# Log-sum rows of a two-pass attention: from four broadcast multiplies on VectorE to one small copy and four transfers

## The chip, the cores and the metric

The kernel runs on one core of a Trainium2 chip. The metric is the device time of one execution in microseconds. Five engines work side by side, each on its own list of instructions in written order: PE (TensorE, matmuls), DVE (VectorE), ACT (ScalarE), POOL (GpSimd) and SP (SyncE, which here only issues transfers). Matmuls write to PSUM, from which DVE and ACT take the results into SBUF. Semaphores order the engines against each other.

## The reference

Two attention layers, "A" and "B", each over its own input of 2048 tokens with 1024 features and 32 heads of 32; their outputs are concatenated.

```
def _B_ref(x, wqkv, wo):                      # "dense" units of the kernel
    B, S, D = x.shape
    H = 32; Dh = D // H; W = 256
    qkv = (x @ wqkv).reshape(B, S, 3, H, Dh).transpose(2, 0, 3, 1, 4)
    q, k, v = qkv[0], qkv[1], qkv[2]
    scores = jnp.einsum("bhqd,bhkd->bhqk", q, k) * (Dh ** -0.5)
    idx = jnp.arange(S)
    mask = (idx[:, None] - idx[None, :] >= 0) & (idx[:, None] - idx[None, :] < W)
    scores = jnp.where(mask[None, None], scores, -1e9)
    p = _softmax(scores, axis=-1)
    o = jnp.einsum("bhqk,bhkd->bhqd", p, v)
    return o.transpose(0, 2, 1, 3).reshape(B, S, D) @ wo
```

A query of layer B sees the last 256 keys, itself included. Layer A differs in the mask alone: a query sees 8 keys, two positions apart (itself, 2 back, ... 14 back). All data is float32.

## The kernel before

The work is cut into 8 units of 512 tokens: units 0 to 3 are layer B ("dense"), units 4 to 7 layer A ("window"). A unit has 8 head groups of 4 heads, numbered `hg = 8 * unit + s`. There are four kinds of work on PE: the projections to queries and keys (L518) and to values (L583), the output projection (L645), together "the gemm"; and attention. For precision, each float32 operand of the gemm is split into a high and a low part (`Stream.parts`, L195: copy at L201 or L204, difference at L207), and three products are summed.

Dense attention of one head group has two passes.

First pass (`first`, L846): for each of 4 heads and 4 blocks of 128 queries, the scores are computed with queries on the partitions (L857), masked and reduced to a maximum by DVE (L862), and put through an exponential on ACT that also sums them (L867). The scores' operands are "stacked": three copies of the 32 head dimensions, high and low parts, fill partitions 0 to 95 of `qst` and `kst`, so one matmul over 96 rows sums the three products.

Log-sum (`log_sum`, L878, and `rows`, L894): logarithm of the sums (L880), maximum minus logarithm (L885), again as high and low parts (L887, L888). One matmul with the identity (L896) turns these into 32 rows of 128 columns in PSUM: row 16a + 4j + b is part a of head j and query block b. `spread` (L898) brings these rows to partitions 96 to 127 of the stacked queries.

Second pass (`second`, L932): the scores are computed again, now with keys on the partitions (L940), and with the log-sum added by the matmul itself, since the contraction also runs over partitions 96 to 127, where the keys hold ones (`ones`, L338, written once at the start). An exponential (L947) gives the finished probabilities; two triangular masks are cut by POOL (L926) or DVE (L929), and the product with the values follows (L987), in two lots of key blocks. The result leaves PSUM at L822 and L826 and feeds the output projection of the unit.

Two copies of `qst` and `kst` alternate between head groups. The stacking transfers of group `hg` (L479, and L408 and L469 for the keys that a unit passes on to the next) wait until the second pass of group `hg - 2` is done. They are issued by SP, from buffers (`natp`, 3 of them) that the projection's results are put in (L455, L459).

The order of all instructions is made by a planner when the kernel is built (L1058 on). It has four lists, log-sum rows, second passes, first passes and gemm, and at each step takes the item that can start first; at a tie attention goes before gemm. Each list is in a fixed order: the gemm cannot skip an item that waits. The planner keeps a clock (`Clock`, L44) for each engine and for the transfers, from a table of durations; `ROWS_LATE`, `KEYS_LATE` and `SEAT_LATE` (L28, L29) are added to the clock times at which certain data is taken to be there. For a transfer by SP the clock books 1.34 us from issue to movement, and for the kind `part` 0.33 us of movement and 0.56 until it is seen (L50 to L54); SP itself is held 0.63 us. What the planner believes sets only the order; on the chip, semaphores set the times.

After the last two dense groups, `qst` and `kst` are taken over as buffers for the window units: `clear` (L808 on) zeroes them on POOL (L810, L814). It is called from `free_keys` (L785), when the last matmul of a second pass has been written. The window units have no log-sum rows; L711 and L774 are their scores and values.

## Time and profile before

| | |
|---|---|
| median of 3 runs | 1832.38 us (1831.74 to 1832.67) |
| profiled execution, span | 1830.6 us |
| PE busy | 1807.8 us (99%) |
| DVE busy | 1202.9 us (66%) |
| ACT busy | 889.4 us (49%) |
| POOL busy | 394.4 us (22%) |
| L902, the four multiplies of `spread` | 128 instructions, 79.3 us of DVE |
| transfers issued by SP | 544 |

The span is the time from the first to the last instruction of the profiled execution, 1.8 us (0.1%) below the median of the runs. PE's busy time covers a matmul from its start to a modelled end; matmuls overlap, so a mean duration of one (394 ns for 512 columns) is longer than the step from one to the next. A group's row has its line, engine, operation, output and inputs, the shapes, the count, then busy time and mean duration of one, then the idle time of the engine just before it and what ended that. "PEld" is the loading of a matmul's stationary operand.

### The profile page before, as it was taken

How to read it: one execution, taken by the hardware profiler on the slowest of the kernel's cores; microseconds unless marked ns; L12 is line 12 of the kernel's file. 1: busy time of each engine (PE TensorE's matmuls, PEld its weight loads, DVE VectorE, ACT ScalarE, POOL GpSimd, SP SyncE). 2: the span in 40 equal slices, each digit the busy share in tenths (PEclk: the TensorE clock that was granted, in tenths of full speed). 3: DMA queues.
4: the chain of work that ended last, by engine and by line, in shares of the span. 5: the costliest groups of instructions: out<-in, count | busy, mean ns of one | idle time of the engine just before them, and what ended most of it. 6: DMA issues, size and time to landing. Idle time of an engine off the chain costs nothing.

```text
span 1830.6 us, 38331 instructions
## 1 busy us (share of the span) xinstructions
PE 1807.8 (99%) x14826; PEld 1477.5 (81%) x14826; DVE 1202.9 (66%) x2694; ACT 889.4 (49%) x2254; POOL 394.4 (22%) x926
## 2 busy tenths in 40 slices
PE   9999999999999999999999999999999999999998
PEld 7787777888778888788887788888888788888887
DVE  6677886768867669777777564655547445655463
ACT  5556466565655655656555343433425234423331
POOL 3322323233242324332233200110001000100000
PEclk9999999999999999999999999999999999999999
DMA  8455665545656456455554343444334443534432
GB/s 242 121 138 139 176 164 150 170 121 160 164 155 164 136 151 183 125 157 141 141 142 130 110 135 116 152 143 130 119 115 143 133 138 108 162 107 128 127 104 83
DMA packets 109141, 257.43 MB, mean 141 GB/s; under 512 B 14496, under 2 KB 29856, under 8 KB 108960
## 3 DMA queue, kind: packets, MB, share of 16 engines
q0 software_dynamic: 41760, 152.06, 28.1%
q1 hardware_dynamic: 56832, 83.00, 17.6%
q10 hardware_dynamic: 10368, 19.93, 3.0%
q8 instruction: 117, 1.92, 0.5%
q14 instruction: 64, 0.52, 0.1%
HBM read 164.63 MB, written 23.07 MB: 103 GB/s over the span
## 4 chain that ended last, share of the span: by engine, by line
PE 92%; DVE 4%; DMA 2%; ACT 2%; issue 1%; SPq 0%; ACTq 0%; POOL 0%; DVEq 0%; POOLq 0%
PE g L518 37%; PE g L645 19%; PE g L583 17%; PE s L940 5%; PE s L857 5%; PE o L987 5%; PE s L711 2%; PE o L774 2%; DMA raw<-xs 1%; DVE w L207 1%; DVE s L862 1%; ACT s L867 0%; DMA qst<-nat 0%; DMA pbuf<-nat 0%; DVE x L207 0%
## 5 line engine op out<-in xcount | busy, mean ns | idle before, releaser
L518 PE MATMUL g<-x,w 128*128 128x512 f32 x3072 | 770.2, 394 | 3.8 <-DVE nm L729 2.4
L518 PEld LDWEIGHTS g<-x,w 128*128 128x128 f32 x3072 | 566.3, 189 | 114.2 <-issue 8.3
L583 PE MATMUL g<-w,x 128*128 128x256 f32 (+1 forms) x2304 | 391.9, 320 | 0.9 <-issue 0.7
L207 DVE TENSOR_TENSOR w<-raw,w 128x512 fp32r<-128x512 f32 x516 | 338.6, 698 | 52.0 <-ACT w L201 44.8
L583 PEld LDWEIGHTS g<-w,x 128*128 128x128 f32 x2304 | 332.3, 190 | 29.2 <-DVE w L207 1.8
L645 PE MATMUL g<-ot,w 128*128 128x512 f32 x1416 | 343.6, 393 | 3.7 <-DVE ot L826 1.8
L867 ACT ACTIVATE s<-s,nm 128x384 f32<-128x384 f32 (+2 forms) x512 | 274.3, 536 | 102.1 <-DVE nm L862 101.8
L862 DVE CUSTOM_DVE_ANT_0 s<-s,mask_d 128x384 f32<-128x384 f32 (+2 forms) x512 | 261.5, 553 | 88.2 <-PE s L857 87.5
L645 PEld LDWEIGHTS g<-ot,w 128*128 128x128 f32 x1416 | 262.4, 188 | 59.3 <-DVE ot L826 3.2
L926 POOL TENSOR_SCALAR_AFFINE_SELECT pbuf<-pbuf 128x128 f32<-128x128 f32 (+1 forms) x606 | 219.8, 391 | 325.1 <-ACT pbuf L947 323.8
L947 ACT ACTIVATE pbuf<-s 128x384 f32<-128x384 f32 (+2 forms) x480 | 202.7, 505 | 72.2 <-PE s L940 70.2
L159 POOL DMA_DIRECT2D raw<-wqk x126 | 68.1, 540 | 457.5 <-DVE w L207 356.3
L204 DVE CAST w<-raw 128x1024 fp32r<-128x1024 f32 x205 | 141.7, 691 | 24.8 <-PE g L518 24.0
L940 PEld LDWEIGHTS s<-qst,kst 128*128 128x128 f32 x704 | 113.0, 188 | 41.2 <-ACT s L867 16.3
L857 PE MATMUL s<-kst,qst 96*128 96x384 f32 (+2 forms) x512 | 142.4, 342 | 0.9 <-ACT s L867 0.6
L940 PE MATMUL s<-qst,kst 128*128 128x256 f32 (+2 forms) x704 | 136.5, 302 | 3.5 <-ACT s L867 3.0
L719 DVE TENSOR_TENSOR band<-s,near 128x160 f32<-128x160 f32 x128 | 32.4, 315 | 158.0 <-PE s L711 158.0
L536 ACT COPY ost<-g 128x512 f32<-128x512 f32 x54 | 31.7, 587 | 207.1 <-PE g L645 200.4
L857 PEld LDWEIGHTS s<-kst,qst 96*128 96x128 f32 x512 | 93.4, 189 | 26.2 <-issue 4.7
L826 DVE TENSOR_TENSOR ot<-o,ot 128x512 fp32r<-128x512 f32 x64 | 44.0, 688 | 101.6 <-ACT ot L822 101.4
L867 ACT ACTIVATION_READ_ACCUMULATOR s<-s,nm 128x1 f32 x512 | 105.3, 206 | 0.0
L159 POOL DMA_DIRECT2D raw<-wo x64 | 34.2, 534 | 304.2 <-DVE w L207 260.2
(77 smaller groups left out, 1298.6 us busy)
## 6 DMA issues: line engine op xcount, KB each, us to landing
raw<-wqk POOLq DMA_DIRECT2D x126, 512.0 KB, 4.3
raw<-wv POOLq DMA_DIRECT2D x72, 512.0 KB, 5.1
raw<-wo POOLq DMA_DIRECT2D x64, 512.0 KB, 4.1
qst<-nat SPq DMA_DIRECT2D x96, 256.0 KB, 5.3
kst<-nat SPq DMA_DIRECT2D x96, 256.0 KB, 5.6
raw<-xs POOLq DMA_DIRECT2D x28, 512.0 KB, 4.6
outs<-ost ACTq DMA_DIRECT2D x56, 256.0 KB, 2.3
kst<-halo SPq DMA_DIRECT2D x72, 128.0 KB, 4.5
```

Source lines behind the costliest of these rows:

```text
L159: (self.nc.scalar if early else self.nc.gpsimd).dma_start(raw if len(ap.shape) == 2 else raw.rearrange("p (a b) -> p a b", a=2), ap)
L204: nc.vector.tensor_copy(t[:, 0, :], raw)
L207: nc.vector.tensor_tensor(t[:, 1, c:c + 512], raw[:, c:c + 512], t[:, 0, c:c + 512].bitcast(F32), op=ALU.subtract)
L518: nc.tensor.matmul(h["ps"], h["w"][:, a, k * P:(k + 1) * P], xt[u][k][:, b, :], start=(k == 0 and i == 0), stop=(k == NK - 1 and i == 2))
L583: nc.tensor.matmul(ps, xt[u][kw * g + k][:, a, p0:p0 + P], h["w"][g][:, c, k], start=(first and t == 0 and half == 0), stop=(last and t == 2),
L645: nc.tensor.matmul(h["ps"], w[:, a, c:c + P], ot[u, k][:, b, :], start=(k == 0 and i == 0), stop=(k == NK - 1 and i == 2))
L857: nc.tensor.matmul(ps[:, :n], q[0:96, j, b * P:(b + 1) * P], kk[0:96, j, c0:c1], start=True, stop=True)
L862: nc.vector.tensor_tensor_reduce(ps[:, :n], ps[:, :n], mask[:, cut:full], scale=-1.0, scalar=BIG, op0=ALU.add, op1=ALU.min, accum_out=nm)
L867: nc.scalar.activation(ps[:, :n], ps[:, :n], AF.Exp, bias=nm, scale=-1.0, accum_out=sm)
L926: nc.gpsimd.affine_select(w, w, pattern=[[0, m], [step, n]], compare_op=ALU.is_ge, fill=0.0, base=base, channel_multiplier=chan)
L940: nc.tensor.matmul(ps[:, i * n:(i + 1) * n], kk[:, j, 256 + kb * P:256 + (kb + 1) * P], q[:, j, q0:q0 + n], start=True, stop=True)
L947: nc.scalar.activation(w, ps[:, :pack * n].rearrange("p (j n) -> p j n", j=pack), AF.Exp)
```

## The change

The rows of the log-sums leave PSUM by one copy of 32 x 128 elements into a new SBUF tile `row`, on ACT or DVE, whichever the planner's clock has free first. The PSUM bank is given back after that copy. Four transfers issued by SP, one for each head slot j, then each write all 32 rows of 128 as 8 rows of 512 (part and head, by 4 query blocks) into partitions 96 to 103 of the stacked queries' slot j. So each head's slot holds the rows of all four heads, where before DVE multiplied each slot by a pattern that left only its own head's row at its own block. The choice of the head moves to the keys: instead of ones in partitions 96 to 127, slot j of the stacked keys holds 1 in the two rows of head j (high and low part) and 0 in the others. The second pass contracts over 104 partitions in place of 128.

`ROWS_LATE` goes from 0 to 2.0: the planner takes the rows to be there 2 us after the transfer's booked landing. `clear` for the last dense group is called later, after its last product with the values has been written.

```
-ROWS_LATE, KEYS_LATE = 0, 1.2
+ROWS_LATE, KEYS_LATE = 2.0, 1.2
...
-        pick = cst["pick"] = pickp.tile([32, 16], F32, name="pick")
+        pick = cst["pick"] = pickp.tile([P, 16], F32, name="pick")[96:104, :4]
         nc.gpsimd.memset(pick, 0.0)
-        for row in (0, 16):
-            nc.gpsimd.affine_select(pick, pick, pattern=[[-1, 16]], compare_op=ALU.not_equal, fill=1.0, base=-row,
+        for row in (0, 4):
+            nc.gpsimd.affine_select(pick, pick, pattern=[[-1, 4]], compare_op=ALU.not_equal, fill=1.0, base=-row,
                                     channel_multiplier=1)
...
         def ones():
-            zero = cst["mask_d"][96:P, None, P:2 * P].to_broadcast([32, 24, P])
+            zero = cst["mask_d"][96:104, None, P:2 * P].to_broadcast([8, 6, P])
             for t in kst:
-                nc.scalar.activation(t[96:P, :, :].rearrange("p j (a s) -> p (j a) s", s=P), zero, AF.Identity,
-                                     bias=1.0, scale=1.0)
-                ck.use("act", 2.7, ck.now)
+                for j in range(4):
+                    nc.scalar.activation(t[96:104, j, :].rearrange("p (a s) -> p a s", s=P), zero, AF.Identity,
+                                         bias=cst["pick"][:, j:j + 1], scale=1.0)
+                    ck.use("act", 0.72, ck.now)
...
-        if hg >= last_dense - 1 and U * NG - 1 > last_dense:
+        if hg == last_dense - 1 and U * NG - 1 > last_dense:
             ck.defer(ck.now + 0.3, lambda: clear(hg % 2))
...
             def spread():
-
-                h["rows"] = []
-                for j in range(4):
-                    nc.vector.tensor_tensor(q[96:P, j, :].rearrange("p (b s) -> p b s", s=P),
-                                            ps[0:32, None, 0:P].to_broadcast([32, 4, P]),
-                                            cst["pick"][0:32, 4 * j:4 * j + 4, None].to_broadcast([32, 4, P]), op=ALU.mult)
-                    e = ck.use("dve", 0.61, ck.now)
-                    h["rows"].append(e + ROWS_LATE)
+                row = rowp.tile([32, P], F32R, tag="row", name="row")
+                if ck.ends("act", 0.22, ck.now) <= ck.ends("dve", 0.2, ck.now):
+                    nc.scalar.copy(row, ps[0:32, 0:P])
+                    e = ck.use("act", 0.22, ck.now)
+                else:
+                    nc.vector.tensor_copy(row, ps[0:32, 0:P])
+                    e = ck.use("dve", 0.2, ck.now)
                 rs.give(bank, e)
+
+                def place():
+                    h["rows"] = []
+                    for j in range(4):
+                        nc.sync.dma_start(q[96:104, j, :].rearrange("r (b s) -> r b s", s=P).bitcast(F32),
+                                          row.bitcast(F32))
+                        h["rows"].append(ck.copy("part", e, ck.now) + ROWS_LATE)
+
+                if hg < 2 or hg - 2 in done["second"]:
+                    place()
+                else:
+                    waiting.setdefault(hg - 2, []).append(place)
...
-                nc.tensor.matmul(ps[:, i * n:(i + 1) * n], kk[:, j, 256 + kb * P:256 + (kb + 1) * P],
-                                 q[:, j, q0:q0 + n], start=True, stop=True)
+                nc.tensor.matmul(ps[:, i * n:(i + 1) * n], kk[0:104, j, 256 + kb * P:256 + (kb + 1) * P],
+                                 q[0:104, j, q0:q0 + n], start=True, stop=True)
...
                 if hg == last_dense and ks[-1] == nk - 1:
+                    if U * NG - 1 > last_dense:
+                        clear(buf)
                     seat_free(hg)
```

More of the change, by code (lines that the diff above doesn't have):

```diff
@@ L229 @@
     pickp = ctx.enter_context(tc.tile_pool(name="pickp", bufs=1))
+    rowp = ctx.enter_context(tc.tile_pool(name="rowp", bufs=1))
     opool = ctx.enter_context(tc.tile_pool(name="opool", bufs=NO))
```

## The prediction

> **What bounds the kernel now.** I read the page's busy table first, then the busy time by stretches of the span, then who waited for whom, and last the timeline at the places where PE was not full.

> ```profile
> span 1830.6 us, 38331 instructions
> PE 1807.8 (99%) x14826; PEld 1477.5 (81%) x14826; DVE 1202.9 (66%) x2694; ACT 889.4 (49%) x2254; POOL 394.4 (22%) x926
> 0.00:1030.00 1030.00, 1018.34 (x6127) 820.91 (x6129) 762.47 (x1954) 596.15 (x1708) 317.18 (x785) 1.00 0.55 151
> 0.00:30.00 30.00, 27.03 (x96) 20.49 (x97) 16.52 (x25) 15.31 (x17) 12.12 (x32) 0.94 0.78 236
> 30.00:60.00 30.00, 29.81 (x139) 23.95 (x138) 23.16 (x76) 18.00 (x64) 6.42 (x17) 1.00 0.60 168
> 150.00:180.00 30.00, 26.86 (x152) 20.76 (x151) 24.18 (x76) 20.77 (x68) 7.11 (x19) 1.00 0.53 139
> 360.00:390.00 30.00, 30.00 (x209) 23.80 (x208) 20.35 (x51) 17.85 (x51) 8.28 (x24) 1.00 0.55 147
> 420.00:450.00 30.00, 30.00 (x204) 26.58 (x203) 27.50 (x64) 13.87 (x41) 8.04 (x16) 1.00 0.55 153
> 450.00:480.00 30.00, 29.04 (x176) 22.58 (x175) 25.99 (x68) 19.20 (x54) 13.62 (x28) 1.00 0.72 201
> 690.00:720.00 30.00, 28.83 (x208) 24.17 (x208) 28.12 (x68) 15.89 (x45) 12.76 (x23) 1.00 0.61 175
> ```

> In the rows of stretches the columns are the stretch, its length, and the busy time of PE, PEld, DVE, ACT and POOL, then PE's clock, the DMA share and GB/s. The dense units, which alone are changed, take the first 1030 us. PE is busy for 1018.34 of them: 11.66 us are idle, and 0.19 + 2.97 = 3.16 of these lie in the first 60 us, where the kernel starts. So an edit that takes work off the other engines can give back about 8.5 us that this view shows. In the middle of a unit (360 to 390) PE has no idle time at all and DVE has 10 us of it. Where one unit goes over into the next (420 to 450, 690 to 720, and 150 to 180 in the first) DVE is the full one: it splits the next unit's input there, and there PE has its few holes.

> [...]

> ```profile
> 1805.13 21.77 PE g L645 x96
> L902 DVE TENSOR_TENSOR qst<-s,pick x128: 672/674/686, 49.5 to 1013.8; 32x512 fp32r<-32x512 f32 x128
> PE s L896 <- DVE hl L888: 3.6, 4, 2.0
> ACT nat L455 <- DMA qst<-nat: 6.1, 3, 2.8
> ```

> The last two are waits: us in total, times, longest. Nobody is listed as waiting for L902, which the change removes. What PE does wait for is the step before it (L888), and an evacuation of PSUM waits for a stacking transfer (L455): there the gemm has run so far ahead that it needs attention to set a buffer free.

> **The change part by part.** *Matmuls.* As many as before, contracting over 104 rows in place of 128. The nearest rows on both sides of 104 are equal, so 0:

> ```profile
> L857 PE MATMUL s<-kst,qst 96*128 96x384 f32 x448 | 129.8, 351 | 0.9 <-ACT s L867 0.6
> L940 PE MATMUL s<-qst,kst 128*128 128x384 f32 x256 | 70.0, 350 | 0.2
> L438 SPq DMA_DIRECT2D pbuf<-nat x256: 467/544/1912, 1030.7 to 1768.8; - x128
> DMA to landing us min/median/max: 2.0/2.9/7.0
> L867 ACT ACTIVATE s<-s,nm 128x128 f32<-128x128 f32 x32 | 10.9, 340 | 13.0 <-DVE nm L862 13.0
> L880 ACT ACTIVATE ln<-sm 128x16 f32<-128x16 f32 x32 | 6.9, 216 | 0.8
> SPq L479 <- PE s L940: 336.0, 28, 27.5
> ```

> *DVE.* 128 instructions of 0.674 us go, four in each of 32 head groups: 2.5 us a group in one piece, 79 us in all (union). In return there is one copy of 32x128 out of PSUM for each group, on ACT or DVE, whichever the planner finds free. The trace has no such copy; it lies between ACT's 0.216 us (16 columns) and 0.340 (128 columns), and I take 0.3. ACT has 40% of its time free in these units: 0.

> *The four transfers.* SP issues 128 more, by L438's median 0.544 us each: 70 us in 1030. SP stood waiting for PE for 336 us in its stacking line alone, so the issue time is hidden. What they add is latency. A 16 KB transfer is not in the trace; the nearest is L438 (64 KB, same queue, also into some partitions of a tile), 2.0 to 7.0 us from issue to landing, median 2.9. I take 2.9 and keep both ends. The planner books 1.34 + 0.33 + 0.56 + 2.0 = 4.23 us from the end of the copy for the first and 0.63 more for each one after it, so PE's written order puts the second-pass scores (L940) later and gemm in the space. If the transfer lands within what is booked, PE loses nothing for as long as there is gemm. Queued behind the four on SP are the next stacking copies; they wait for the end of this very second pass (hg minus 2), so they are not delayed further by the queue.

> Where the gemm is held by attention, the longer path counts. Four places:

> ```profile
> 430.13 0.22 PE L896 MATMUL s<-ident,hl 128*32 128x128 f32 x1
> 432.74 0.34 PE L940 MATMUL s<-qst,kst 128*128 128x128 f32 x2
> 444.87 0.29 DVE L929 TENSOR_TENSOR pbuf<-pbuf,keep_d 128x128 f32<-128x128 f32 x1
> 494.53 0.22 PE L896 MATMUL s<-ident,hl 128*32 128x128 f32 x1
> 496.88 2.48 DVE L902 TENSOR_TENSOR qst<-s,pick 32x512 fp32r<-32x512 f32 x4
> 499.98 0.33 PE L940 MATMUL s<-qst,kst 128*128 128x128 f32 x2
> 1011.78 0.22 PE L896 MATMUL s<-ident,hl 128*32 128x128 f32 x1
> 1013.99 0.33 PE L940 MATMUL s<-qst,kst 128*128 128x128 f32 x2
> 1026.90 0.94 POOL L810 MEMSET band<- 128x1024 f32 x1
> 1027.79 1.91 POOL L814 MEMSET wide<- 128x2176 f32 x1
> 1029.66 1.11 POOL L926 TENSOR_SCALAR_AFFINE_SELECT pbuf<-pbuf 128x256 f32<-128x256 f32 x3
> 1031.92 0.50 PE L645 MATMUL g<-ot,w 128*128 128x512 f32 x1 [0.69 <-ACT ot L822]
> 160.17 0.22 PE L896 MATMUL s<-ident,hl 128*32 128x128 f32 x1
> 163.30 0.34 PE L940 MATMUL s<-qst,kst 128*128 128x384 f32 x1
> 178.47 0.22 PE L896 MATMUL s<-ident,hl 128*32 128x128 f32 x1 [1.99 <-DVE hl L888]
> ```

> From the rows matmul to the first paired second-pass matmul the new plan needs about 0.22 + 0.2 + 0.3 + 0.15 + 4.23 + 0.63 = 5.7 us (0.2 and 0.15 are the planner's own allowances), and 5.1 where the first item has one head, as in the first unit.
> (a) Head group 13, just before a unit's end: 2.6 us now, 3.1 more then. But its first masks come at 444.87, long after its exponentials, since DVE is full; they wait for DVE, which has 2.5 us less to do. Hidden: 0. The same at group 21.
> (b) Groups 15 and 23, whose output the next o-projection waits for: 5.45 us now, as L902 itself stands behind other DVE work until 496.88; 0.2 more then. 0.
> (c) Group 31: 2.2 us now, 3.5 more. Against that, the two memsets (0.94 + 1.91 = 2.85 us) no longer stand in front of its last three masks on POOL. Net 0.6, and PE already waits 0.7 there: +1.
> (d) The first unit, where attention and not gemm leads: group 4 takes 3.1 us now, 1.9 more then, and the next group on the same buffers follows it. +2, with at least 0 (DVE is 2.5 us shorter for each group, too) and at most 2 x 3.5 = +7.

> *What the lighter DVE gives back.* PE waits for L888, behind DVE's queue, 3.6 us in all, 2.0 of them at 178.47. I take 2.5 of these; the ends are 0 and the whole 8.5 us of idle time.

> *Other edits.* The rows' PSUM bank is free some 2 us sooner (bounded by the same 8.5 us; not counted twice). The constant rows of the keys take eight short ACT instructions in place of two at 24 us, where ACT is half idle: 0. The last memset comes later, but the windowed group that needs it starts after others: 0.

> The sum: 1830.6 + 1 + 2 - 2.5 = 1831.1 us for a profiled execution. The median of the runs shown, 1832.4, lies 1.8 above this profile; 1833 us is predicted. Less than 0.2% of the time, 3.7 us, is about what a measurement of this kernel can tell from no change.

> **The rivals.** *Slower: row transfers land later than booked.* PE executes in written order, so a late row stops the gemm behind it too. It happens where the rows come while the 256 KB stacking copies are still moving. Seven copies were issued from 455.24 to 460.06 and group 14's rows matmul ran at 462.93:

> ```profile
> 455.24 1.95 SPq L479 DMA_DIRECT2D qst<-nat  x3
> 460.06 0.54 SPq L469 DMA_DIRECT2D halo<-nat  x1
> 462.93 0.22 PE L896 MATMUL s<-ident,hl 128*32 128x128 f32 x1 [0.31 <-DVE hl L888]
> halo<-nat SPq DMA_DIRECT2D x1, 256.0 KB, 9.1
> ```

> The last of the seven landed 9.1 us after its issue, at 469.2, while the rows would be issued at 463.5. A transfer that needs 7.0 us in place of 2.9 lands 7.0 - 4.2 = 2.8 us after its booked time; at four unit ends 11 us, 1844 us in all. It decides once lateness at those places is over 0.9 us each. For it: the same queue and such traffic at each unit end. Against it: the planner counts the queue in its own clock, and in mid-unit the copies are done (360 to 390 has a DMA share of 0.55). [...]

> *Faster: DVE at the unit ends was the true limit.* With 2.5 us less of it in front of the input splits, masks and first-pass reductions, the holes close: at most the 8.5 us, with the +3 above hidden as well, so 1832.4 - 6 = 1826 with about two thirds given back. For it: DVE 27.5 and 28.12 of 30 us at two unit ends. Against it: PE lost only 0.96 and 1.17 us in the stretches around them.

> *No effect at all:* PE was full and stays full, and the small losses and gains cancel. This is the forecast, since DVE is off the path everywhere but at the unit ends.

> **How the numbers follow.** Within 0.2% (1829 to 1836): 0.38. Slower, by late rows: 0.35. Faster, by the DVE relief: 0.27. The range runs from 1823, near the floor set by the idle time, to 1848, the slower rival with two thirds as much again of its 11 us and a little; that leaves out some 0.05 below and 0.11 above. For the forecast alone it is 1829 to 1836.

> **What would show it.** Right: DVE's busy time in the dense units 80 us lower, L940's mean unchanged, SP with 128 more issues, and PE idle in the first 1030 us still 9 to 14 us. The slower rival: a wait of PE, or of its weight loads, on the transfer that writes qst from the row tile, above all at unit ends. The faster rival: PE idle at 150 to 180 us down from 3.1 us to about 1. Wrong in another way: since every booked time moves, the planner may write quite another order of PE's work, and holes may arise in places that now have none; the view of stretches would show them away from the four places above.

## The result and the profile after

The changed kernel takes 1857.3 us (median of 4 runs, 1855.2 to 1861.8) beside 1832.1 us of the kernel before in the same comparison. The ratio is 1.0142, with a 95% interval of 1.0128 to 1.0156: slower by 25 us, where 1833 us had been predicted, and outside the range that ended at 1848. In the changed kernel's own numbering L898 is the rows matmul, L903 and L906 are the new copy on ACT and DVE, L913 the four transfers, L953 the second-pass scores, L859 the first-pass scores, L520 and L585 the projections.

The page's span and busy table after:

```profile
span 1855.2 us, 38489 instructions
PE 1820.9 (98%) x14826; PEld 1484.4 (80%) x14826; DVE 1127.2 (61%) x2571; ACT 888.9 (48%) x2265; POOL 386.2 (21%) x948
```

DVE lost 1202.9 - 1127.2 = 75.7 us of work, and nobody gained by it. PE, with the same 14826 matmuls, is busy 13.1 us longer and idle 34.3 - 22.8 = 11.5 us longer. The busy time by stretches shows where. Columns: stretch, length, busy time of PE, PEld, DVE, ACT and POOL, then PE's clock, DMA share, GB/s. After:

```profile
0.00:1055.00 1055.00, 1031.53 (x6119) 827.72 (x6119) 686.00 (x1831) 595.43 (x1719) 308.20 (x809) 0.99 0.55 150
1055.00:1855.00 800.00, 789.39 (x8708) 656.67 (x8707) 441.21 (x740) 293.44 (x546) 78.01 (x140) 1.00 0.42 127
180.00:210.00 30.00, 26.55 (x172) 22.98 (x170) 22.55 (x61) 12.09 (x38) 9.04 (x19) 0.94 0.60 165
360.00:390.00 30.00, 29.02 (x170) 22.92 (x162) 18.09 (x48) 17.90 (x53) 6.58 (x19) 1.00 0.51 138
450.00:480.00 30.00, 27.41 (x175) 21.92 (x174) 23.73 (x59) 17.00 (x48) 12.09 (x24) 0.95 0.61 168
720.00:750.00 30.00, 27.41 (x154) 20.98 (x153) 21.52 (x59) 14.72 (x44) 7.06 (x15) 0.94 0.63 170
```

and the kernel before, its last 800 us:

```profile
1030.00:1830.00 800.00, 789.44 (x8703) 656.57 (x8697) 440.45 (x740) 293.20 (x546) 77.20 (x142) 1.00 0.42 127
```

The window units are the same to 0.1 us, so all of it lies in the dense units, which now end some 25 us later: 23.5 us of idle PE there in place of 11.7, and 1031.5 us of busy time in place of 1018.3. The holes are small and in many places. The loss grows unit by unit: measured at the evacuation of each unit's last keys, the kernel is 3.9, 10.7, 16.6 and 25.0 us behind the kernel before, and it ends 24.6 behind.

Who waits for whom: PE's waits for attention's work in the changed kernel, a selection (us in total, times, longest):

```profile
PE s L898 <- DVE hl L890: 4.2, 4, 1.9
PE s L859 <- DMA kst<-nat: 3.0, 2, 1.8
PE s L859 <- ACT s L869: 2.5, 4, 0.9
PE s L953 <- ACT s L869: 2.0, 1, 2.0
PE s L859 <- DMA qst<-row: 1.0, 1, 1.0
```

The new transfers are waited for once, for 1.0 us. What has changed is the order. PE's timeline at group 13, and SP's at the same time; the columns are start, length, engine, line, operation and, in brackets, the idle time before:

```profile
440.14 0.22 PE L898 MATMUL s<-ident,hl 128*32 128x128 f32 x1
440.20 1.62 PE L520 MATMUL g<-x,w 128*128 128x512 f32 x6
441.65 1.60 PE L585 MATMUL g<-w,x 128*128 128x256 f32 x12
443.09 0.86 PE L859 MATMUL s<-kst,qst 96*128 96x384 f32 x4
443.79 6.64 PE L585 MATMUL g<-w,x 128*128 128x256 f32 x54
450.26 0.56 PE L953 MATMUL s<-qst,kst 104*128 104x128 f32 x4
```

```profile
440.71 2.96 SPq L913 DMA_DIRECT2D qst<-row  x4
```

From the rows matmul to the second pass it is 450.26 - 440.14 = 10.1 us, in place of 2.6 before. PE stands still for none of it: four first-pass matmuls and 72 of the gemm (6 + 12 + 54) were written into the space. Over all 32 head groups, counted in the two traces, this way is 9.0 us on the mean in place of 3.3.

The other part of the loss is PE's clock. Stretches of 10 us in the changed kernel:

```profile
190.00:200.00 10.00, 7.98 (x44) 7.40 (x43) 8.60 (x26) 4.76 (x17) 4.10 (x7) 0.83 0.42 131
220.00:230.00 10.00, 10.00 (x44) 8.30 (x44) 7.75 (x27) 5.08 (x20) 0.83 (x2) 0.83 0.42 129
470.00:480.00 10.00, 8.06 (x48) 5.77 (x48) 7.72 (x20) 4.22 (x13) 1.77 (x2) 0.85 1.03 261
740.00:750.00 10.00, 10.00 (x40) 8.34 (x39) 7.35 (x18) 2.82 (x9) 1.61 (x2) 0.84 0.67 193
790.00:800.00 10.00, 9.52 (x54) 6.00 (x50) 5.44 (x19) 6.20 (x18) 3.57 (x11) 0.89 0.48 125
```

A clock of 0.83 over 10 us is 1.7 us of full clock lost. Behind each row stands one slot of 3.4 us at clock 0.50, from 193.7, 221.0, 477.0, 739.8 and 797.8; three of the rows cut their slot off. Five slots make 5 x 1.7 = 8.5 us. Apart from these, each of the two kernels has one such slot in the first 20 us, and the kernel before has no other in its dense units. So 11.8 us of the 25 are idle time and about 8.5 are matmuls at half the clock. Some 5 us are left, which lie in PE's busy time. Part of them comes with the pauses: the dense units have some 41 in place of 24, and before each the last matmul is counted as busy to its modelled end, 0.394 - 0.227 = 0.17 us beyond the step to the next (0.394 is the page's mean of one of 512 columns, 0.227 the 21.77 us of the 96 at the end of the kernel before, by 96), which makes an estimated 2.9 us. Of the last 2 the cause isn't known.

### The profile page after: what moved, and what is told of

Read it like the earlier page. It is cut to its first block, busy times and chain, and to the rows that moved or that the text cites. A ratio compares the mean times of both kernels' runs of the same rounds, so it can differ in the third digit from the quotient of the medians.

```text
span 1855.2 us, 38489 instructions
## 1 busy us (share of the span) xinstructions
PE 1820.9 (98%) x14826; PEld 1484.4 (80%) x14826; DVE 1127.2 (61%) x2571; ACT 888.9 (48%) x2265; POOL 386.2 (21%) x948
## 4 chain that ended last, share of the span: by engine, by line
PE 90%; DMA 3%; DVE 3%; ACT 2%; issue 1%; SPq 0%; ACTq 0%; POOL 0%; DVEq 0%; POOLq 0%
PE g L520 36%; PE g L647 18%; PE g L585 17%; PE s L953 5%; PE s L859 5%; PE o L1000 4%; PE s L713 2%; PE o L776 2%; DMA raw<-xs 1%; ACT s L869 1%; DMA kst<-nat 1%; DVE w L207 1%; DVE s L864 1%; DMA halo<-nat 0%; ACT pbuf L960 0%
## 5 line engine op out<-in xcount | busy, mean ns | idle before, releaser
L520 PE MATMUL g<-x,w 128*128 128x512 f32 x3072 | 768.7, 394 | 2.9 <-ACT x L201 2.3
L520 PEld LDWEIGHTS g<-x,w 128*128 128x128 f32 x3072 | 566.7, 188 | 115.6 <-issue 7.4
L585 PE MATMUL g<-w,x 128*128 128x256 f32 (+1 forms) x2304 | 395.5, 323 | 2.4 <-issue 2.3
L585 PEld LDWEIGHTS g<-w,x 128*128 128x128 f32 x2304 | 338.1, 192 | 31.7 <-issue 3.1
L939 POOL TENSOR_SCALAR_AFFINE_SELECT pbuf<-pbuf 128x128 f32<-128x128 f32 (+1 forms) x628 | 210.3, 364 | 270.6 <-ACT pbuf L960 269.2
L859 PE MATMUL s<-kst,qst 96*128 96x384 f32 (+2 forms) x512 | 141.4, 346 | 8.4 <-DMA kst<-nat 3.0
L953 PEld LDWEIGHTS s<-qst,kst 104*128 104x128 f32 x704 | 113.1, 190 | 41.5 <-ACT s L869 14.5
L953 PE MATMUL s<-qst,kst 104*128 104x256 f32 (+2 forms) x704 | 137.3, 304 | 4.1 <-ACT s L869 2.0
L859 PEld LDWEIGHTS s<-kst,qst 96*128 96x128 f32 x512 | 93.5, 190 | 35.0 <-issue 7.8
L159 POOL DMA_DIRECT2D raw<-wv x72 | 46.8, 650 | 232.7 <-DVE w L207 173.6
## 6 DMA issues: line engine op xcount, KB each, us to landing
qst<-nat SPq DMA_DIRECT2D x96, 256.0 KB
kst<-nat SPq DMA_DIRECT2D x96, 256.0 KB
outs<-ost ACTq DMA_DIRECT2D x56, 256.0 KB
```

The lines of the kernel that those rows point to most:

```text
L159: (self.nc.scalar if early else self.nc.gpsimd).dma_start(raw if len(ap.shape) == 2 else raw.rearrange("p (a b) -> p a b", a=2), ap)
L520: nc.tensor.matmul(h["ps"], h["w"][:, a, k * P:(k + 1) * P], xt[u][k][:, b, :], start=(k == 0 and i == 0), stop=(k == NK - 1 and i == 2))
L585: nc.tensor.matmul(ps, xt[u][kw * g + k][:, a, p0:p0 + P], h["w"][g][:, c, k], start=(first and t == 0 and half == 0), stop=(last and t == 2),
L859: nc.tensor.matmul(ps[:, :n], q[0:96, j, b * P:(b + 1) * P], kk[0:96, j, c0:c1], start=True, stop=True)
L939: nc.gpsimd.affine_select(w, w, pattern=[[0, m], [step, n]], compare_op=ALU.is_ge, fill=0.0, base=base, channel_multiplier=chan)
L953: nc.tensor.matmul(ps[:, i * n:(i + 1) * n], kk[0:104, j, 256 + kb * P:256 + (kb + 1) * P], q[0:104, j, q0:q0 + n], start=True, stop=True)
```

## The experiments

Three theories were set against each other. **A:** the longer way from the rows to the second pass costs, already because the planner books it and writes PE's order by it. **B:** the transfers themselves cost: they land late, or they hold up the stacking copies behind them on SP. **C:** the order of the kernel before happens to be a very good one, and any wide rewriting loses 20 to 40 us. The medians of the kernel before beside them were between 1829.5 and 1832.8 us; each ratio is to its own.

| run | what it is | median, us | ratio (95% interval) |
|---|---|---|---|
| b_late05 | before, rows booked 0.5 us late | 1858.5 | 1.0155 (1.0140 to 1.0171) |
| b_late2 | 2.0 us late | 1862.2 | 1.0168 (1.0151 to 1.0186) |
| b_late6 | 6.0 us late | 1870.6 | 1.0217 (1.0197 to 1.0238) |
| b_neg05 | 0.5 us early | 1837.2 | 1.0028 (1.0015 to 1.0041) |
| b_keys17 | keys booked 0.5 us later | 1837.0 | 1.0025 (1.0013 to 1.0037) |
| b_mask25 | mask choice shifted | 1831.4 | 0.9995 (0.9985 to 1.0005) |
| b_mid2 | 2.0 us late, groups s = 1 to 4 | 1841.4 | 1.0052 (1.0034 to 1.0069) |
| b_end2 | 2.0 us late, groups s = 0, 5, 6, 7 | 1845.8 | 1.0075 (1.0055 to 1.0095) |
| b_late2_nox | b_late2, lighter DVE | 1857.9 | 1.0146 (1.0129 to 1.0163) |
| b_late2_hold | b_late2, second pass gets its turn | 1856.1 | 1.0124 (1.0109 to 1.0139) |
| b_relief | before, 3 of 4 multiplies left out | 1833.2 | 1.0022 (1.0007 to 1.0037) |
| b_clear | before, late `clear` alone | 1829.6 | 0.9999 (0.9989 to 1.0008) |
| after | the change | 1857.3 | 1.0142 (1.0128 to 1.0156) |
| a_late0 | after, `ROWS_LATE` 0 | 1852.8 | 1.0119 (1.0104 to 1.0134) |
| a_early | after's transfers in before's order | 1915.8 | 1.0475 (1.0459 to 1.0491) |
| a_actq | after, rows issued by ACT | 1887.8 | 1.0302 (1.0278 to 1.0325) |
| a_nodma | after, transfers left out | 1858.2 | 1.0154 (1.0136 to 1.0172) |
| a_hold | after, second pass gets its turn | 1870.4 | 1.0214 (1.0190 to 1.0237) |
| n1 | key-side pattern without transfers | 1859.1 | 1.0165 (1.0150 to 1.0180) |

### Booking alone, and other places for the transfers

b_late2 and b_late6 are the kernel before, multiplies and all, with one constant changed. a_late0 changes it back in the changed kernel. a_actq moves the four transfers to ACT's queue.

```
b_late2:  -ROWS_LATE, KEYS_LATE = 0, 1.2
          +ROWS_LATE, KEYS_LATE = 2.0, 1.2      (b_late6: 6.0)
a_late0:  -ROWS_LATE, KEYS_LATE = 2.0, 1.2
          +ROWS_LATE, KEYS_LATE = 0, 1.2
a_actq:   -    nc.sync.dma_start(q[96:104, j, :]...
          -    h["rows"].append(ck.copy("part", e, ck.now) + ROWS_LATE)
          +    nc.scalar.dma_start(q[96:104, j, :]...
          +    h["rows"].append(ck.load("part", e, ck.now) + ROWS_LATE)
```

> The kernel before with one edit: ROWS_LATE 2.0 in place of 0. Nothing is transferred and no instruction is added; the planner merely takes the log-sum rows to be there 2 us later. Theory A (the lost time comes from the longer way from the rows matmul to the second pass, whether booked or real): the changed kernel lost 25 us with some 7 us more on that way, so 2 us should cost about 7 us: 1839. Theory B (the transfers do it: they hold up SP's queue and the stacking copies): none here, 1832 within 3. Theory C (this tuned order loses with any disturbance of the planner): a loss of 5 to 25 us that has no relation to the 2 us.

> The kernel before with ROWS_LATE 6.0, about as late as the second pass stands in the changed kernel's trace (7 to 10 us from the rows matmul, 2 to 5 before). Theory A: about the loss of the changed kernel, 1850 to 1858, and more than with 2.0. Theory B: 1832 within 3. Theory C: a loss like that with 2.0, with no order between the two.

> The changed kernel with ROWS_LATE 0: the four transfers as they are, but the planner takes the rows to be there as soon as its clock books the landing, 2 us sooner. Theory A: if the booking sets the delay, about 7 us are won, 1850; if the transfers land later than booked, PE waits in order for them and part of it is lost again, with waits of PE on the transfer from the row tile of 1 us and more. Theory B: no gain, 1857 or slower. Theory C: a change of some us either way.

> The changed kernel with the four transfers issued by ACT in place of SP (and so booked by the planner on ACT's clock), ROWS_LATE 2.0 as in the change. The row transfers no longer stand behind the stacking copies in SP's list. Theory A: the delay gets shorter where SP was busy (head groups 5 and 7 took 14 to 16 us in the changed kernel), by 1 to 2 us elsewhere: 1845 to 1852. Theory B: most of the loss goes, 1835 to 1842. Theory C: 5 to 25 us above 1832, no relation.

b_late2 has no new transfer, no changed DVE and no changed key, and it loses at least as much as the whole change: the booking alone is enough. That speaks against B. A had the sign and not the size: it put b_late2 at 1839 and b_late6 at 1850 to 1858. b_late2's lag behind the kernel before grows in steps at the unit ends, at the keys of the next unit's first group: 0.1 to 8.4 us, 9.8 to 19.0, and 22 to 29 at the end of the last dense unit, with 1 to 3 us between one step and the next. PE's timeline of b_late2 at group 13:

```profile
429.96 0.22 PE L896 MATMUL s<-ident,hl 128*32 128x128 f32 x1
430.02 0.74 PE L857 MATMUL s<-kst,qst 96*128 96x384 f32 x3
...
435.04 0.44 PE L940 MATMUL s<-qst,kst 128*128 128x128 f32 x2
435.32 0.93 PE L583 MATMUL g<-w,x 128*128 128x256 f32 x6
436.08 0.63 PE L940 MATMUL s<-qst,kst 128*128 128x128 f32 x4
436.55 7.36 PE L583 MATMUL g<-w,x 128*128 128x256 f32 x60
443.74 0.93 PE L940 MATMUL s<-qst,kst 128*128 128x256 f32 x5
...
454.41 1.00 PE L857 MATMUL s<-kst,qst 96*128 96x384 f32 x2 [1.25 <-ACT s L867]
...
467.90 1.00 PE L857 MATMUL s<-kst,qst 96*128 96x384 f32 x2 [0.44 <-ACT s L867]
...
471.68 0.29 PE L896 MATMUL s<-ident,hl 128*32 128x128 f32 x1 [2.77 <-DVE hl L888]
```

Two microseconds of booking became a second pass that is interrupted for 7.4 us of gemm and ends at 463.7, where it ended at 455.2 in the kernel before; the rows matmul of the next group, at 462.93 before, runs at 471.68, after PE has stood for 2.77 us. The clock falls there, too:

```profile
456.00:459.40 3.40, 3.40 (x17) 1.95 (x10) 2.77 (x7) 1.17 (x4) 0.56 (x3) 0.50 0.02 5
469.70:476.50 6.80, 4.82 (x12) 3.85 (x13) 4.96 (x11) 1.77 (x6) 0.00 (x0) 0.50 0.54 128
```

The pauses shown are 1.25 + 0.44 + 2.77 us, against 0.61 + 0.31 in the kernel before at the same place, so 3.5 us more; and PE's 3.40 + 4.82 us of work at half the clock would have taken 4.1 us less at the full one, by an estimate that goes by these two figures and the clock alone. Together they are most of the step of 8.3 us. a_late0 shows the other side: with less booked, PE does run into the transfers (9.7 us in 9 waits), and the kernel is only 4.6 us better than the change. a_actq lost another 30 us to ACT's queue, which no theory had foreseen (the highest of them ended at 1857), with waits of PE on ACT's exponentials and on the keys' stacking:

```profile
PE s L859 <- DMA kst<-nat: 12.4, 5, 4.3
PE s L859 <- ACT s L869: 9.8, 14, 1.5
```

### Single parts of the change

b_relief leaves three of the four multiplies of each group out, with their rows of the queries zeroed once, so three heads get no log-sum; all bookings, and so PE's order, stay. b_clear moves only `clear` to where the change has it. a_early puts the change's copy and transfers into the kernel before's order, booked like the multiplies. n1 has the pattern on the keys, and four scaled block copies on ACT or DVE in place of the transfers, booked to the end of the last for all heads.

```
b_relief: +    if j == 0: nc.vector.tensor_tensor(q[96:P, j, :]...
b_clear:  -    if hg >= last_dense - 1 and U * NG - 1 > last_dense:
          +    if hg == last_dense - 1 and U * NG - 1 > last_dense:
          ...
          +    clear(buf)          (after the last product with the values)
a_early:  +    nc.vector.tensor_copy(row, ps[0:32, 0:P])
          +    for j in range(4):
          +        nc.sync.dma_start(q[96:104, j, :]..., row...)
          +        e = ck.use("dve", 0.61, ck.now)
          +        h["rows"].append(e + ROWS_LATE)          (ROWS_LATE 0)
n1:       +    for b in range(4):
          +        out = q[96:P, :, b * P:(b + 1) * P]
          +        src = ps[0:32, None, 0:P].to_broadcast([32, 4, P])
          +        nc.scalar.activation(out, src, AF.Copy, scale=cst["pickb"][:, b:b + 1])
          ...
          +        nc.vector.tensor_tensor(out, src, cst["pickb"][:, b:b + 1, None]..., op=ALU.mult)
          +    h["rows"] = [e + ROWS_LATE] * 4              (ROWS_LATE 0)
```

> The kernel before with three of the four multiplies of each head group left out (the log-sum rows of three heads in four stay zero, so their probabilities are not normalised), while the planner still books all four: PE's order is that of before, row for row, and DVE does 60 us less. It measures the lighter DVE by itself. If DVE at the unit ends is a limit in the order of before: up to 8 us faster, 1824 to 1828. If PE's list alone sets the time: 1830 to 1832.

> The kernel before with one part of the change alone: the zeroing for the last dense group is called after its last product with the values. PE's order stays that of before. All theories: within 1.5 us of before; the 2.85 us of memsets leave POOL ahead of three masks, and PE waited 0.7 us there.

> The changed kernel's copy and four transfers, but booked in the planner like the four multiplies of before, so that PE's order is that of before, row for row. What it loses is the transfers' true lateness, paid in PE's waits. Theory A (the way's length costs, booked or real): the second pass stands 2 to 5 us after the rows matmul in this order and the rows land 4 to 5 us after it (12 where SP is busy), so 1 to 3 us for each of 32 groups: 1865 to 1900, with the waits of PE on the transfer from the row tile adding up to about that. If only a changed order costs, and not lateness: 1840 or less.

> The key-side head pattern without transfers: for each query block one scaled copy from PSUM writes that block of all four heads' slots at once (32 partitions as before, contraction over 128), on ACT or on DVE, whichever the planner has free first. No latency is added and DVE gets some of its 79 us off. Theory A: the second pass comes as early as before or earlier, so 1826 to 1834. Theory C (any other order loses): 1840 to 1860.

b_relief: 58 us less of DVE (1144.6 busy in place of 1202.9) in the same order of PE is worth nothing. b_clear: no difference. a_early: with the order of the kernel before, the transfers are late at nearly every group. PE's waits for them (another 14.0 us fall on its weight loads):

```profile
PE s L942 <- DMA qst<-row: 52.4, 31, 4.6
```

So the way by transfers really is longer than by multiplies, by up to 4.6 us, and unless it is booked it costs 86 us. n1 loses 30 us without having the transfers, where A had put it at 1826 to 1834 and C at 1840 to 1860. It books the last copy's end for all heads, but its way hardly grew: counted in the trace over the 32 groups, it is 3.4 us on the mean, in place of 3.3 in the kernel before. So n1 speaks for C and against a loss that goes by the length of the way.

### The order or the transfers

a_nodma is the changed kernel without the four transfers (the constant rows of the queries are zeroed once, the probabilities are not normalised); all bookings, and so the orders of PE and DVE, stay. The others are controls of the kernel before: half a microsecond of booking, and a constant that has nothing to do with the rows. b_late2_nox takes 30 us of work off DVE in b_late2, without touching PE's order: from unit 2 on the low parts of the input aren't formed, and the gemm reads the high part twice.

```
a_nodma:     -    nc.sync.dma_start(q[96:104, j, :]..., row...)
b_late05:    +ROWS_LATE, KEYS_LATE = 0.5, 1.2
b_mask25:    -MASK_BIAS = 0.2
             +MASK_BIAS = 0.25
b_late2_nox: +    if not skip: nc.vector.tensor_tensor(t[:, 1, c:c + 512], ..., op=ALU.subtract)
             +    xt[u][k][:, b if u < 2 else 0, :]
```

> The changed kernel with its four transfers of each head group left out; the constant rows 96 to 103 of the stacked queries are zeroed once at the start, so the probabilities are not normalised. The planner still books the transfers, so PE and DVE keep the order of the changed kernel exactly. If the written order is what costs (theory C), 1852 to 1857 us, as the changed kernel. If transfers that land later than booked, or the copies queued behind them on SP, cost the 25 us, the time falls to 1840 or less, with the two-microsecond stops of PE at unit ends gone.

> The kernel before with ROWS_LATE 0.5 in place of 0, nothing else: the planner writes the second pass of each group half a microsecond later. If the loss grows with the booked lateness (theory A: 30 us at 2.0 and 38 at 6.0), about 1837 us. If any order other than that of the kernel before costs a full 20 to 40 us (theory C), 1850 to 1865.

> The kernel before with MASK_BIAS 0.25 in place of 0.2, which only shifts the choice between POOL and DVE for a mask now and then and has nothing to do with the log-sum rows. Theory A (lateness of the rows): within 5 us of the kernel before, 1829 to 1834. Theory C (any other order costs): 1845 to 1860.

> The kernel before with ROWS_LATE 2.0 (1862 us, lost at three unit ends in steps of 7.5 to 9 us), PE's order unchanged, but from unit 2 on DVE's low-part differences of the dense input are left out and the gemm reads the high part in their place (less precise). If the later second pass costs so much because DVE is full of input splitting at a unit's end, the steps at the unit ends 1, 2 and 3 shrink to 3 us or less each: about 1842. If it is the order of PE alone, 1860.

a_nodma decides against B. Its busy table:

```profile
PE 1820.2 (98%) x14826; PEld 1483.6 (80%) x14826; DVE 1126.5 (61%) x2571; ACT 888.4 (48%) x2265; POOL 389.1 (21%) x950
```

The same PE, DVE and ACT as with the transfers, PE's order the same in both traces but for 4 of the 14826 matmuls, and the same time within the intervals: over the whole kernel, the 128 transfers, their issues on SP and their traffic cost nothing that can be measured here. (In its profile a_nodma is 3.5 us ahead of the change at the last keys of units 1 and 2, and level at those of unit 3, after 10.2 us at clock 0.50 from 792.3.) The lighter DVE and the late `clear` were worth nothing by themselves, so the written order costs the 25 us.

b_mask25 cost nothing, which C hadn't foreseen, but it rewrote far less of PE's order than the others, and that in the first 450 us alone. b_late05, which A put at 1837, came out where C had it: most of the loss is there with the first half microsecond, and it is no straight line from there to 2.0 and 6.0. Its way is 3.6 us on the mean, 0.3 more than before; b_late2's is 5.4. The two controls pointed to different theories, so wider ones followed. b_late2_nox came out at 1858, near the 1860 that it was to have if PE's order alone is the cause, and not at 1842. Its steps at the unit ends are the ones of b_late2 (5.3 to 13.4 us and 14.5 to 23.7), and so is the pause before the rows matmul:

```profile
476.99 0.22 PE L898 MATMUL s<-ident,hl 128*32 128x128 f32 x1 [2.78 <-DVE hl L890]
```

DVE, full of input splitting at the unit ends, was thought to be what makes a later second pass dear. With that work partly gone and the order kept (it is the same in both traces, matmul by matmul), the steps stay: DVE's splitting isn't the cause there, the order is.

### Any other order, and where

b_keys17 and b_neg05 rewrite PE's order about as widely as b_late05 (1504 and 1758 lines of difference from the kernel before, against 1607) without a later second pass. The traces limit this for b_keys17: nine tenths of its differences in PE's list lie in the first 450 us, and from unit 2 on its order is nearly that of before, so it says little about the later unit ends. b_neg05's go on to 900 us. b_mid2 and b_end2 book 2.0 us in one half of the groups each.

```
b_keys17: +ROWS_LATE, KEYS_LATE = 0, 1.7
b_neg05:  +ROWS_LATE, KEYS_LATE = -0.5, 1.2
b_mid2:   +    h["rows"].append(e + (2.0 if 1 <= hg % 8 <= 4 else 0))
b_end2:   +    h["rows"].append(e + (0 if 1 <= hg % 8 <= 4 else 2.0))
```

> The kernel before with KEYS_LATE 1.7 in place of 1.2: the planner takes stacked keys of the dense units to be there 0.5 us later; nothing is booked later on the way from the rows to the second pass. PE's order is rewritten about as widely as by ROWS_LATE 0.5 (1504 lines of difference against 1607). Theory C (any wide rewriting of the order costs): 1845 to 1865 us. Theory A (only later second passes cost): 1828 to 1836.

> The kernel before with ROWS_LATE -0.5 in place of 0: the planner takes the rows to be there half a microsecond before the multiplies end, so each second pass is written a little earlier and PE may stand for up to 0.5 us at a group. PE's order is rewritten widely (1758 lines). Theory C: 1845 to 1865 us. Theory A: 1826 to 1840, with the waits of PE on the multiplies (L902) the only loss.

> The kernel before with ROWS_LATE 2.0 for the head groups s = 1 to 4 of each dense unit alone and 0 for the others. If the loss of 30 us is made where units go over into each other, 1830 to 1838 us here. Theory C: 1845 to 1865, here and in the next run alike.

> The kernel before with ROWS_LATE 2.0 for the head groups s = 0, 5, 6 and 7 of each dense unit alone and 0 for the others. If the loss is made where units go over into each other, nearly all of it is here: 1852 to 1863 us, in steps of 6 to 9 us at units 1, 2 and 3's ends.

C falls in the form given, that any wide rewriting loses 20 to 40 us: b_neg05 and b_keys17 cost 5 us each (b_neg05 within A's range, b_keys17 1 us above it). That some orders lose and others don't, whatever they book, isn't ruled out by so few. b_keys17's dense units have a PE as full as before:

```profile
0.00:1030.00 1030.00, 1016.52 (x6113) 820.70 (x6114) 766.41 (x1961) 596.59 (x1706) 320.45 (x778) 1.00 0.54 151
```

Every kernel before that books all groups' rows later, by 0.5 us or by 6, loses 26 to 39 us. b_mid2 and b_end2 split the loss, 9 and 13 us of 30. The expectation that all of it belongs to the groups near a unit's end failed in both: b_mid2 came out 3 us above its range and b_end2 6 us below. But in b_mid2, too, PE pauses at the unit ends (1.25 and 0.96 us of waiting for a bank of scores at each of the three), so what is booked late in mid-unit is at least in part paid where units meet. One mark goes with the loss in these traces: at groups 13, 21 and 29, just before the unit ends, it takes 25 us from the rows matmul to the end of the second-pass scores in the kernel before, no more in b_keys17 and b_neg05, but 26 to 34 us in the change, n1, b_mid2, b_end2 and the three runs that book all groups later. It shows where time goes, not why.

### Giving the second pass its turn

In b_late2, first-pass items are written between the rows and the second pass. Both runs here add a rule to the planner: no first-pass item is written when the first scores of a second pass are ready within 2.1 us (b_late2_hold) or 4.5 us (a_hold).

```
+        soon = twos[pos["2"]].ready() if ... and twos[pos["2"]] in heads else None
         for name, seq in seqs.items():
...
+            if name == "1" and soon is not None and soon <= ck.now + 2.1:
+                continue
```

> The kernel before with ROWS_LATE 2.0 (1862 us), and one rule more in the planner: where the first scores of a dense group's second pass will be ready within 2.1 us, no first-pass item is written before them; gemm fills the time. If the booked lateness costs because first-pass items take the score banks in that gap and the second pass then falls behind them, most of the 30 us comes back: 1833 to 1845. If the longer way itself costs, whatever stands in the gap, 1855 or more.

> The changed kernel with the same rule, for 4.5 us ahead of the first second-pass scores. If first-pass items taking the banks are the cause, 1835 to 1847 us in place of 1857. If the longer way itself costs, 1855 or more, since the first pass is now held up by up to 4.5 us in each group.

Neither came back to 1847 or less; both lie at 1855 or more, where they were to be if lost turns aren't the whole cause. b_late2_hold is 6 us faster than b_late2: its steps at the ends of units 1 and 2 went from 8.3 and 9.2 us to 4.6 and 3.9, but it loses in mid-unit much of what it won. a_hold is 13 us slower than the change. Lost turns explain a part of the steps at two unit ends and not the loss as a whole.

**What stays open.** Shown is that the order costs it, and that later booking of the rows alone is enough to make such an order. Not shown is that lateness is what makes an order bad: b_late05 and n1 lose as much as the change with a way 0.3 and 0.1 us longer than before, and a_late0 with a way of 6.9 us loses 21, less than either. The order of before may simply be a rare good one. Which feature of an order does it isn't shown either: DVE's splitting and the second pass's turn were tried and are not it by themselves. Whether a booking between 0 and 0.5 us has a threshold wasn't tried. No run beat the kernel before.

## Why the prediction was wrong

- **Matmuls over 104 rows, 0:** right. The 104x384 form takes 355 ns, against 350 over 128 rows. The rows of the groups in the changed kernel:

```profile
L953 PE MATMUL s<-qst,kst 104*128 104x384 f32 x256 | 71.8, 355 | 2.2 <-ACT s L869 2.0
L906 DVE CAST row<-s 32x128 fp32r<-32x128 f32 x22 | 6.1, 279 | 19.2 <-PE s L898 18.7 <-DMA kst<-nat 0.4
L903 ACT CAST row<-s 32x128 fp32r<-32x128 f32 x10 | 2.5, 254 | 13.0 <-PE s L898 13.0
```

- **The copy, 0.3 us:** right, 0.25 and 0.28.
- **DVE 79 us lighter, 2.5 of them given back:** the first right (75.7 with the new copies), the second wrong. b_relief gives back nothing, and the wait for `hl`, from which the 2.5 was taken, is 4.2 us after the change in place of 3.6.
- **The transfers:** that SP's issues cost PE nothing was right, though four take 2.96 us at SP and not 4 x 0.544 = 2.2; a_nodma prices issues, landings and traffic at nothing. The rival of late landings, 1844 us, had the sign and not the cause: PE waited 1.0 us for a row transfer. The copies do stand in front of the rows on SP. At group 5, SP's timeline has the four transfers 4.5 us behind the rows matmul of 177.22:

```profile
177.14 1.90 SPq L481 DMA_DIRECT2D qst<-nat  x3
179.13 1.88 SPq L481 DMA_DIRECT2D kst<-nat  x3
181.06 0.61 SPq L471 DMA_DIRECT2D halo<-nat  x1
181.76 2.91 SPq L913 DMA_DIRECT2D qst<-row  x4
```

  The planner's clock has such a queue in it, and so wrote the second pass later still. This is order at the issuing engine. Behind it the transfers wait once more: the rows' packets, which alone in the trace have 512 bytes, start 1.4 us after the issue at group 13, and at group 14, issued at 476.69, only 3.3 us after it, at 479.98, when the 256 KB copies ahead of them have moved and the last of these (to `halo`) is ending, at 480.47. The rows' last packet ends at 480.87, and group 14's second pass is written 11.2 us behind its rows matmul of 476.13, so nobody waits there.
- **"PE loses nothing for as long as there is gemm":** this is the step that failed. Gemm did fill the way, as the timeline of group 13 shows, and the time was lost all the same. The prediction treated the order as given, with the second pass slid some us to the right, and searched four places for a wait. The planner instead wrote a different order for all dense units: "(a) Hidden: 0" became a way of 10.1 us, not 5.7, and the cost came as 1 to 2 us pauses and half the clock in places that had been full (11.8 us more idle, about 8.5 us at half clock). That it costs without any late transfer is shown by b_late2 (1862 us) and a_nodma (1858 us).
- **(b) groups 15 and 23, 0; (c) group 31, +1; (d) first unit, +2 with 0 to 7:** (b) was too low. The output projection waits 0.78 + 0.22 us for group 15's output, at 538.57 and 539.29, in place of 0.23 before, and the lag grows from 10.5 to 14.2 us between unit 2's second keys and third queries, the stretch where that output is used; at group 23 it grows from 16.7 to 22.1. The lag moved by -0.4 us after the last dense keys and by 3.6 over the first unit and its switch, near what (c) and (d) said. The rest of the loss lies between these places.
- **The range:** its upper end was built from late landings at four places (and 1848 is about a third of the 11 us above 1844, not two thirds). The sentence that would have held the result, that the planner "may write quite another order of PE's work", stood at the end with no price and no chance.

## What to carry to other kernels

Where a planner writes the order, a latency that is booked is not free because other work fills it: change that one number in the old kernel first and run it, since here 0.5 us of booking alone cost as much as the whole change. Any edit that touches the bookings also draws a new order, so the edit and its order have to be measured apart, as b_relief (new work, old order) and b_late2 (old work, new order) do. Taking work off an engine that nobody waited for gained nothing here (58 us of DVE in b_relief). And look at the granted clock beside the idle time: in the changed kernel a pause of PE of 1.94 us, with the clock at 0.50 behind it, cost 1.94 + 1.6 us, nearly twice its length.

## What was not expected of the hardware

Behind a pause of PE of 1.94 us its granted clock was 0.50 for 3.4 us. PE's timeline of the changed kernel, where unit 1 goes over into unit 2:

```profile
476.13 0.22 PE L898 MATMUL s<-ident,hl 128*32 128x128 f32 x1 [1.94 <-DVE hl L890]
476.19 0.91 PE L520 MATMUL g<-x,w 128*128 128x512 f32 x3
476.93 5.41 PE L585 MATMUL g<-w,x 128*128 128x512 f32 x16
```

and the clock in that place:

```profile
477.00:480.40 3.40, 3.40 (x10) 2.66 (x9) 3.33 (x6) 0.60 (x1) 1.05 (x1) 0.50 0.91 270
```

The 16 matmuls take 5.41 us in place of 16 x 0.227 + 0.17 = 3.80 (the last one is counted to its modelled end): 1.6 us lost, on top of the 1.94 us pause. The lower clock doesn't follow every pause. The kernel before has one of 1.99 us at 178.47 (quoted in the prediction) and keeps its clock, 1.00; b_mask25 has the same pause of 2.00 us a little later and doesn't, 0.83. First the kernel before, then b_mask25:

```profile
176.00:186.00 10.00, 8.01 (x63) 7.60 (x62) 8.35 (x16) 5.65 (x15) 5.00 (x8) 1.00 0.65 141
```

```profile
180.50 0.22 PE L896 MATMUL s<-ident,hl 128*32 128x128 f32 x1 [2.00 <-DVE hl L888]
...
180.00:190.00 10.00, 9.50 (x64) 9.53 (x65) 9.39 (x17) 3.99 (x9) 5.75 (x10) 0.83 0.44 98
```
